# Batch 0 goes from its first to its second stage inside SBUF: twelve small DMAs in place of a round trip through DRAM

## Chip, cores, metric

One core of one Trainium2 chip. The metric is device time in microseconds (us) of one execution. Engines: PE (TensorE, matmuls), DVE (VectorE), ACT (ScalarE), POOL (GpSimd) and SP (SyncE). SP and ACT issue DMAs on their own queues, POOL issues DMAs[...] (the page calls its queue software_dynamic).

## The reference

An FFT over the sequence and over the model dimension, of which the real part is kept, and then a mixture of experts in which each token goes to the one expert with the largest logit.

```python
B, S, D = 8, 2496, 256
x = np.fft.fft(np.fft.fft(x, axis=1), axis=2).real      # per batch
x = x.reshape(B * S, D)                                  # 19968 tokens
logits = x @ w_gate                                      # 8 experts
e = argmax(logits); g = softmax(logits)[e]               # one expert per token
y = g * (relu(x @ w1[e]) @ w2[e])                        # 256 -> 1024 -> 256
```

Tokens are sorted by expert, computed in groups and put back in their places.

## The kernel before

**Stages of a batch.** The length 2496 is split as 104 x 24. The host lays x out so that batch b comes in three loads x(b,q), q = 0 to 2, each 112 rows of 8 KB (896 KB) into a tile `xq`, of which there are three. The *first* stage (`first`) folds mirrored inputs on DVE (an add, L306, and `fold_d`, L295 to L297), and multiplies with the waves `w1` on PE: twelve positions s, four to a load, each an `s` matmul pair of about 104x112 by 104x256 (`half1`; two s share a PSUM tile, ACT copies it into `t1`, L321). The last s needs two tiles, xq and `pm0`. A `t1` of four s is written to DRAM (`Td`, L342, 448 KB), and when all three are there, `regroup` (L354) reads them back in two halves, `t4`, with other rows on the partitions (768 and 640 KB, in rows of 1 KB).

The *second* stage (`second`) starts with `turn_last` (a small matmul `pr` on `t4`, put back into it by ACT, L372), then eleven groups (`p` matmul pairs of `t4` with the constant m2 from `table`, copied to `zz` by ACT, L379) and ten windows of 128 tokens (two `p` matmuls of `zz`, ACT copies `zs` and `lg`, DVE makes `rows`, L410, two of them for each window). After each five windows `route` (L424 to L455) finds the expert and the place of every token (`oh`, the prefix-sum matmuls `rk`, then `pos` and `pi`). The rows then wait in a queue, and `send` writes one set of 128 rows to the sorted array Xs in DRAM by an indirect DMA on POOL (L236, 20 of them for a batch; the short name here is scatter).

**Experts.** `plan` works out on DVE which blocks of a batch are full, SP reads its table and loads weights (`fetch_weights`, 1 MB each for w1 and w2, three buffers each) and rows (`fetch_rows`, `xb` from Xs). `turn` transposes xb (L584, `xT`), then PE runs the `ph` matmuls (xT by w1) and the `py` matmuls (hT by w2). The block list starts with two blocks of 256 rows and four of 128 that need batch 0 alone.

**Order.** The order on each engine is written out by hand: a generator is advanced step by step, and what a step issues stands in each engine's queue at that place. `first(0)` runs alone. Then batch 1's first stage is advanced by `early` (a generator `ahead_of(1)`: twelve steps of `first(1)`, then its regroups): seven steps ahead of `second(0)` and one on every other step of it. Then the experts' generator runs; whenever it yields without work, one step of the side work is issued (planning of batch 0 and what is left of `early`, then batch 2's first and batch 1's second stage). Ahead of the first `turn` it yields nine times, so that nine such steps precede it:

```python
                for _ in range(9):
                    yield 0, False
                for xT in turn(b, size, xbs[0][0]):
                    pass
```

At the head (L949 to L976) ACT loads waves 0 to 3, and SP in this order: x(0,0), x(0,1), the other waves, x(0,2), `table`, `rt`, `wg`, then x(1,0), x(1,1), the regroups of batch 0, x(1,2), `bt` and the padding of Xs. `rt` and `wg` are multiplied (`pg`) into the routing constants.

Of the kernel before, what the change touches and what calls it, by code (L numbers as in the profile page):

```python
# [12 lines left out]
F32 = mybir.dt.float32  # L13
BF16 = mybir.dt.bfloat16
I32 = mybir.dt.int32
ALU = mybir.AluOpType
# [4 lines left out]
B, S, D = 8, 2496, 256  # L21
# [10 lines left out]
HW = NW // 2  # L32
HALF = -(-NG // 2)
LAST = NW * 128 - (NG - 1) * GP
NT = B * S
E, F = 8, 1024
FC = F // 128
# [178 lines left out]
def kernel(ctx: ExitStack, tc, x, w_gate, w1, w2, out):  # L216
# [3 lines left out]
    def mm(o, lhsT, rhs, start=True, stop=True, **kw):  # L220
        nc.tensor.matmul(o, lhsT=lhsT, rhs=rhs, start=start, stop=stop, **kw)  # L221
# [57 lines left out]
    wg = cp.tile([128, 2, E], F32, name="wg")  # L279
    tri = cp.tile([128, 128], BF16, name="tri16")  # L280
    ones = cp.tile([128, 128], BF16, name="ones16")
    waves = const_dram("w1", consts["w1"])

    def load(b, q):

        if b < B:
            xq = xp.tile([NP, 8, D], F32, tag="xq", name="xq", bufs=3)
            row = (b * NQ + q) * NA
            nc.sync.dma_start(out=xq[:].rearrange("p j d -> p (j d)"), in_=x[row:row + NP])
            ahead[b, q] = xq[0:NA]  # L290

    def fold_d(o, a, n):

# [28 lines left out]

    ahead = {}

    def first(b):

        pm0 = xp.tile([NA, D], F32, tag="pm0", name="pm0")
        for q in range(NQ + 1):
            f = iter(())
            if q < NQ:  # L330
                xq = ahead.pop((b, q))
                f = fold(xq, q, pm0[:])
            next(f, None)
            yield
            if q:
                t1 = xp.tile([NP, 4, D], F32, tag="t1", name="t1")
                half1(b, q - 1, 0, pm, pm0, t1)
# [11 lines left out]
    base = con["cap"]  # L349

    def regroup(b, h):
        t4 = sp.tile([128, HALF, D], F32, tag="t4", name="t4")
        n = min(HALF, NG - h * HALF)
        nc.sync.dma_start(  # L354
            out=t4[:, 0:n], in_=bass.AP(Td[b].tensor, Td[b].offset + h * HALF * GP * D,
                                        [[D, 128], [GP * D, n], [1, D]]))
        ahead[b, "t4", h] = t4

    zz = cp.tile([128, 2, NW * 128], F32, name="zz")

    def second(b):
# [368 lines left out]
    def experts(todo):  # L730
# [44 lines left out]
        for k, (b, size, last, at) in enumerate(todo):  # L775
            n, m = size // 128, BIG // size
            if not k:
                while todo[0][:3] not in tabs:
                    yield 0, False
                fetch_some(0, 1)  # L780
                while b not in whole:
                    yield 0, True
                fetch_some(0)
                for _ in range(9):
                    yield 0, False
                for xT in turn(b, size, xbs[0][0]):
                    pass
# [142 lines left out]
    def ahead_of(b):  # L930

        yield from first(b)
        regroup(b, 0)
        regroup(b, 1)

    def mixed(b):

# [9 lines left out]
        yield from through(b)  # L947

    vec.memset(ones[:], 1.0)  # L949
    act.dma_start(out=con["w1"][:, 0:4], in_=waves[:, 0:4])  # L950
    load(0, 0)
    load(0, 1)
    nc.sync.dma_start(out=con["w1"][:, 4:], in_=waves[:, 4:])
    load(0, 2)
    nc.sync.dma_start(out=table[:], in_=const_dram("table", packed))
    nc.sync.dma_start(out=con["rt"][:], in_=const_dram("rt", consts["rt"]))
    nc.sync.dma_start(out=wg[:], in_=w_gate)
    for k in range(WARM):
        pw = pse.tile([128, D], F32, tag="bd"[k % 2], name="py")
        mm(pw[:], ones[:], bc(ones[:], 1, 2))  # L960
# [120 lines left out]
```

## Time and profile before

| | us |
|---|---|
| median of three runs | 1260.61 (1259.76 to 1261.67) |
| the profiled execution | 1258.56 |
| its span, first to last instruction | 1256.8 |
| PE busy in the span | 1208.1 (96%) |
| DVE, ACT, POOL busy | 759.6, 431.3, 447.5 |
| mean granted clock of PE | 0.976 |
| moved by DMA | 249.79 MB, 199 GB/s |

PE is close to full over the span, so the table alone says little of where an edit can act; the page's slices and the windows say in which part of the span PE has room. In the views below, a row of the timeline is start, duration, engine, line, operation, output and input, and in brackets the idle time ahead of it with what ended it; a row of the chain of waits is start, duration and what the time went to; a row of the windows is the stretch, its length, the busy times of PE, PE's weight loads, DVE, ACT and POOL, then the granted clock, the busy share of the DMA engines and GB/s.

### The profile page before, as it was taken

The page shows a single profiled execution, that of the slowest core. Times are in us where ns is not written, and L with a number is a line of the kernel's source. Part 1 is how long each engine was busy: PE and PEld are TensorE (multiplying, and loading weights), DVE is VectorE, ACT ScalarE, POOL GpSimd, SP SyncE. Part 2 cuts the span into 40 slices and gives each one's busy share as a digit, 9 for nine tenths or more (in the row PEclk, how much of TensorE's full clock was granted, in tenths as well). Part 3 has the DMA queues.
Part 4 walks back from the last instruction along what each step waited for, and adds up shares of the span by engine and source line. Part 5 has one row for each costly group of instructions (what it writes and reads, how often), then busy time and mean ns, then how long its engine had stood idle before and what let it go on. Part 6 is the DMA issues. An engine that isn't in the chain of part 4 may idle for free.

```text
span 1256.8 us, 22295 instructions
## 1 busy us (share of the span) xinstructions
PE 1208.1 (96%) x7289; PEld 1076.3 (86%) x7289; DVE 759.6 (60%) x1804; ACT 431.3 (34%) x1167; POOL 447.5 (36%) x527
## 2 busy tenths in 40 slices
PE   5759999999999999999999999999999999999997
PEld 3648998777788899888988899889999999999996
DVE  3455434343456788566866578686888784444653
ACT  1424332333243433434343333442333332222222
POOL 0154527054117522472226603472364241111112
PEclk6869999999999999999999999999999999999998
DMA  8859899873548434673336435453347237878787
GB/s 235 261 174 350 308 317 311 221 237 122 154 153 263 151 110 163 184 234 116 102 124 211 138 96 162 138 180 101 106 139 206 94 105 284 277 285 284 280 292 284
DMA packets 163216, 249.79 MB, mean 199 GB/s; under 512 B 118601, under 2 KB 130227, under 8 KB 143516
## 3 DMA queue, kind: packets, MB, share of 16 engines
q1 hardware_dynamic: 146327, 203.28, 50.7%
q0 software_dynamic: 15888, 42.14, 9.1%
q10 hardware_dynamic: 885, 2.94, 0.7%
q8 instruction: 59, 0.97, 0.3%
q14 instruction: 57, 0.47, 0.1%
HBM read 194.91 MB, written 54.83 MB: 199 GB/s over the span
## 4 chain that ended last, share of the span: by engine, by line
PE 82%; DVE 9%; DMA 4%; ACT 2%; issue 2%; POOL 0%; SPq 0%; POOLq 0%; DVEq 0%; ACTq 0%
PE py L221 25%; PE ph L221 13%; PE a L221 11%; PE c L221 9%; PE p L221 6%; PE b L221 6%; PE d L221 5%; PE e L221 4%; PE s L221 3%; DMA xq<-in_x_dram 1%; DVE xT L584 1%; DMA Td<-t 1%; DVE y L684 1%; DMA Xs<-rows,pi 1%; DVE hT L639 1%
## 5 line engine op out<-in xcount | busy, mean ns | idle before, releaser
L236 POOL DMA_INDIRECT out_dram<-y,ro x163 | 161.4, 990 | 625.3 <-ACT y L680 301.3
L221 PE MATMUL py<-w_sb,hT 128*128 128x256 f32 x1504 | 339.5, 379 | 0.0
L221 PEld LDWEIGHTS py<-w_sb,hT 128*128 128x128 f32 x1504 | 281.4, 190 | 36.9 <-issue 1.0
L236 POOL DMA_INDIRECT Xs<-rows,pi x160 | 162.4, 1015 | 112.0 <-DVE rows L410 56.7
L221 PE MATMUL ph<-xT,w_sb 128*128 128x128 f32 (+2 forms) x992 | 171.1, 328 | 11.2 <-DVE xT L584 11.1
L221 PEld LDWEIGHTS ph<-xT,w_sb 128*128 128x128 f32 x992 | 136.3, 192 | 35.1 <-issue 16.8
L410 DVE SCALAR_TENSOR_TENSOR rows<-p,zs 128x129 f32<-128x129 f32 x160 | 48.9, 348 | 128.8 <-ACT lg L408 124.8
L221 PE MATMUL a<-xT,w_sb 128*128 128x256 f32 (+1 forms) x512 | 117.8, 357 | 0.0
L838 DVE TENSOR_SCALAR hT<-ph 128x512 f32<-128x512 f32 x43 | 29.7, 691 | 123.7 <-PE ph L221 63.7
L587 ACT ACTIVATE xT<-xT 128x256 f32<-128x256 f32 (+1 forms) x94 | 36.5, 388 | 179.2 <-DVE xT L584 140.8
L221 PEld LDWEIGHTS a<-xT,w_sb 128*128 128x128 f32 x512 | 88.6, 190 | 9.7
L892 ACT ACTIVATE y<-py,xb 128x256 f32<-128x256 f32 x94 | 44.6, 475 | 152.2 <-PE py L221 152.2
L636 DVE TENSOR_TENSOR hT<-hT,b 128x512 f32<-128x512 f32 x57 | 39.2, 688 | 75.7 <-PE b L221 50.0
L646 ACT ACTIVATE hT<-a 128x512 f32<-128x512 f32 x57 | 34.0, 597 | 134.1 <-PE a L221 131.1
L221 PE MATMUL s<-xq,w 104*112 104x256 f32 (+2 forms) x208 | 62.8, 425 | 16.3 <-DVE xq L297 12.1
L469 POOL CAST pi<-due 128x1 int32<-128x1 f32 x140 | 45.1, 322 | 65.5 <-ACT due L468 65.5
L221 PE MATMUL a<-w_sb,hT 128*128 128x128 f32 x528 | 66.0, 276 | 0.0
L221 PEld LDWEIGHTS a<-w_sb,hT 128*128 128x128 f32 x528 | 63.1, 192 | 0.7
L221 PEld LDWEIGHTS p<-table,t 120*128 120x128 f32 x352 | 53.6, 202 | 10.6 <-ACT t L372 2.8
L221 PE MATMUL c<-xT,ws 128*128 128x256 f32 (+1 forms) x256 | 60.3, 362 | 1.0 <-DVE hT L642 0.2
L221 PEld LDWEIGHTS s<-xq,w 104*112 104x112 f32 x208 | 38.5, 204 | 26.3 <-DVE xq L297 10.8
L584 DVE STREAM_TRANSPOSE xT<-xb 128x512 f32<-128x512 f32 (+1 forms) x91 | 56.2, 631 | 7.6 <-DMA xb<-Xs 7.6
(149 smaller groups left out, 2072.6 us busy)
## 6 DMA issues: line engine op xcount, KB each, us to landing
w_sb<-in_moe_w_dram SPq DMA_DIRECT2D x132, 1024.0 KB
xq<-in_x_dram SPq DMA_DIRECT2D x24, 896.0 KB
xb<-Xs SPq DMA_DIRECT2D x112, 128.0 KB
Td<-t SPq DMA_DIRECT2D x18, 448.0 KB
t<-Td SPq DMA_DIRECT2D x8, 768.0 KB
t<-Td SPq DMA_DIRECT2D x8, 640.0 KB
xb<-Xs SPq DMA_DIRECT2D x52, 64.0 KB
xb<-Xs SPq DMA_DIRECT2D x88, 32.0 KB
```

The costliest lines, as they stand in the source:

```text
L221: nc.tensor.matmul(o, lhsT=lhsT, rhs=rhs, start=start, stop=stop, **kw)
L236: return unordered(pool.indirect_dma_start(out=dst, out_offset=bass.IndirectOffsetOnAxis(ap=idx, axis=0), in_=rows, in_offset=None, bounds ...
L410: vec.scalar_tensor_tensor(rows[:, k + m, 0:NY], p3[:, 0:NY], zs[:, 0:1], zs[:, 1:], op0=ALU.add, op1=op)
L469: pool.tensor_copy(idx, due[:])
L584: vec.transpose(free(xT[:], 256 * h, [32, n // 32], [BIG, 2], [1, 32]), free(xb, 512 * h, [64, n // 32], [1, 2], [2, 32]))
L587: act.activation(odd, odd, ACTF.Copy, scale=-1.0)
L636: vec.tensor_tensor(h12, h11, b[:], op=add)
L639: vec.tensor_tensor(h21, h12, d[:], op=add)
L646: act.activation(h11, a[:], ACTF.Relu)
L684: vec.tensor_tensor(o, o, p[:], op=add)
L838: vec.tensor_scalar(o, ph[:], 0.0, None, op0=ALU.max)
L892: act.activation(y[:, i % 2], py[:], ACTF.Copy, scale=meta[:, i, 1:2])
```

## The change

1. Batch 0 has its own first stage, `first_whole`, in half loads (two s at a time: half the add, half the fold, two s). Its waves come in another column order (`wp`, 110 columns, in a buffer of the second weights), so that row r of the result belongs to group r % 11. For each s one DMA on ACT's queue (the last on SP's) then takes `t1` straight to its place in `t4s`: ten partitions, s, s + 12, ..., each with eleven rows of 1 KB. `Td` and the regroups of batch 0 are gone.
2. `t4s`, one tile with both halves, takes the place of the two `t4` buffers for all batches.
3. The waves in their old order, which batches 1 to 7 use, are made from `wp` by three copies on POOL (`natural`), and the two unused columns are set to zero by DVE.
4. The waves come in three parts and x(0,2) in two, in turn on SP. `table`, `rt` and `wg` move to POOL's queue, behind a copy (`came`) that waits for the last waves. x(1,0), x(1,1), `bt` and the padding also move to POOL's queue; x(1,2) stays on SP.
5. `early` gives three steps ahead of `second(0)`, not seven, and inside it none until its fifth step (k = 4). x(2,2) is loaded after the regroups of batch 1, not in `first(1)`.
6. Twelve steps, not nine, precede the first `turn`.

```diff
+NR = 2 * NU * NG
...
-    waves = const_dram("w1", consts["w1"])
+    wp = bp.tile([128, NS + 3, NR], F32, tag="w2", name="wp", bufs=3)[0:NA]
+    order = consts["w1"][:, :, 0:NR].reshape(NA, NS + 3, NG, 2 * NU).swapaxes(2, 3)
+    waves = const_dram("w1", order.reshape(NA, NS + 3, NR))
...
+    def first_whole():
+        pm0 = xp.tile([NA, D], F32, tag="pm0", name="pm0")
+        for q in range(NQ):
+            xq = ahead.pop((0, q))
+            t1 = xp.tile([NP, 4, D], F32, tag="t1", name="t1")
+            for lo in (0, 2):
+                end = q == NQ - 1 and lo
+                a, m = xq[:, lo:lo + 2], xq[:, 4 + lo:6 + lo]
+                n = 2
+                if end:
+                    n = 1
+                    fold_d(pm0[:], m[:, 1], 1)
+                vec.tensor_tensor(a[:, 0:n], a[:, 0:n], m[:, 0:n], op=ALU.add)
+                fold_d(m, a, 2)
+                ps = pm_.tile([NP, 2, D], F32, tag="m", name="s1")
+                for i in range(2):
+                    s = 4 * q + lo + i
+                    o = ps[0:NR, i]
+                    if s < NS - 1:
+                        mm(o, columns(s), m[:, i])
+                        continue
...
+                if end:
+                    for i in range(2):
+                        act.copy(t1[0:NR, lo + i], ps[0:NR, i])
+                else:
+                    act.copy(t1[0:NR, lo:lo + 2], ps[0:NR])
+                for i in range(2):
+                    s = 4 * q + lo + i
+                    (nc.sync if s == NS - 1 else act).dma_start(out=t4s[s:GP:NS, 0:NG], in_=t1[0:NR, lo + i])
+            load(1, q, queue=nc.sync if q == NQ - 1 else pool)
+        for h in range(2):
+            ahead[0, "t4", h] = t4s[:, h * HALF:(h + 1) * HALF]
...
+    def natural(lo, hi):
+        n = hi - lo
+        pool.tensor_copy(free(con["w1"][:, lo:hi], 0, [NP, n], [2 * NU, NG], [1, 2 * NU]),
+                 free(wp[:, lo:hi], 0, [NR, n], [1, NG], [NG, 2 * NU]))
...
-                if b:
+                if b > 1 or b and q < NQ:
                     load(b + 1, q - 1)
...
-        t4 = sp.tile([128, HALF, D], F32, tag="t4", name="t4")
+        t4 = t4s[:, h * HALF:(h + 1) * HALF]
...
-                for _ in range(9):
+                for _ in range(12):
                     yield 0, False
...
         regroup(b, 1)
+        if b == 1:
+            load(b + 1, NQ - 1)
...
-    act.dma_start(out=con["w1"][:, 0:4], in_=waves[:, 0:4])
+    vec.memset(con["w1"][:, :, NR:], 0.0)
+    act.dma_start(out=wp[:, 0:4], in_=waves[:, 0:4])
     load(0, 0)
     load(0, 1)
-    nc.sync.dma_start(out=con["w1"][:, 4:], in_=waves[:, 4:])
-    load(0, 2)
-    nc.sync.dma_start(out=table[:], in_=const_dram("table", packed))
-    nc.sync.dma_start(out=con["rt"][:], in_=const_dram("rt", consts["rt"]))
-    nc.sync.dma_start(out=wg[:], in_=w_gate)
+    nc.sync.dma_start(out=wp[:, 4:8], in_=waves[:, 4:8])
+    rest = load(0, 2, 2)
+    next(rest)
+    nc.sync.dma_start(out=wp[:, 8:], in_=waves[:, 8:])
+    next(rest)
+    came = cp.tile([1, 1], F32, name="came")
+    pool.tensor_copy(came[:], wp[0:1, NS + 2, 0:1])
+    pool.dma_start(out=table[:], in_=const_dram("table", packed))
+    pool.dma_start(out=con["rt"][:], in_=const_dram("rt", consts["rt"]))
+    pool.dma_start(out=wg[:], in_=w_gate)
...
-    for _ in first(0):
-        pass
-    load(1, 0)
-    load(1, 1)
-    regroup(0, 0)
-    regroup(0, 1)
-    load(1, 2)
-    nc.sync.dma_start(out=bt[:], in_=const_dram("blocks", cv))
-    sent(unordered(nc.sync.dma_start(
+    first_whole()
+    pool.dma_start(out=bt[:], in_=const_dram("blocks", cv))
+    sent(unordered(pool.dma_start(
...
+    for lo in range(0, NS + 3, 5):
+        natural(lo, lo + 5)
...
-    for _ in range(7):
+    for _ in range(3):
         next(early)
     for k, _ in enumerate(second(0)):
-        if k % 2 == 0:
+        if k > 3 and k % 2 == 0:
             next(early, None)
```

More of the change, by code (lines that the diff above doesn't have):

```diff
@@ L281, with load @@
     ones = cp.tile([128, 128], BF16, name="ones16")
-    waves = const_dram("w1", consts["w1"])
-    def load(b, q):
+    wp = bp.tile([128, NS + 3, NR], F32, tag="w2", name="wp", bufs=3)[0:NA]
+    order = consts["w1"][:, :, 0:NR].reshape(NA, NS + 3, NG, 2 * NU).swapaxes(2, 3)
+    waves = const_dram("w1", order.reshape(NA, NS + 3, NR))
+    def load(b, q, parts=1, queue=nc.sync):
         if b < B:
@@ L288, in load, with pieces @@
             row = (b * NQ + q) * NA
-            nc.sync.dma_start(out=xq[:].rearrange("p j d -> p (j d)"), in_=x[row:row + NP])
             ahead[b, q] = xq[0:NA]
+            if parts == 1:
+                queue.dma_start(out=xq[:].rearrange("p j d -> p (j d)"), in_=x[row:row + NP])
+                return iter(())
+            return pieces(xq, row)
+    def pieces(xq, row):
+            for k in range(2):
+                nc.sync.dma_start(
+                    out=xq[:].rearrange("p (c j) d -> p c j d", c=2)[:, :, 2 * k:2 * k + 2],
+                    in_=x[row:row + NP].rearrange("p (c j d) -> p c j d", c=2, d=D)[:, :, 2 * k:2 * k + 2])
+                yield
     def fold_d(o, a, n):
@@ L323, with columns @@
     ahead = {}
+    def first_whole():
[19 more added lines that the diff above has]
+                        continue
+                    for k, l, r in ((NS - 1, 0, H + 1), (NS + 1, H + 1, D)):
+                        mm(o[:, l:r], columns(k), pm0[:, l:r], True, False)
+                        mm(o[:, l:r], columns(k + 1), m[:, 1, l:r], False, True)
+                if end:
[9 more added lines that the diff above has]
+            ahead[0, "t4", h] = t4s[:, h * HALF:(h + 1) * HALF]
+    def columns(s):
+        return wp[:, s]
+    def natural(lo, hi):
+        n = hi - lo
+        pool.tensor_copy(free(con["w1"][:, lo:hi], 0, [NP, n], [2 * NU, NG], [1, 2 * NU]),
+                 free(wp[:, lo:hi], 0, [NR, n], [1, NG], [NG, 2 * NU]))
     def first(b):
@@ L357, in regroup @@
         ahead[b, "t4", h] = t4
+    t4s = cp.tile([128, 2 * HALF, D], F32, name="t4s")
     zz = cp.tile([128, 2, NW * 128], F32, name="zz")
```

## Prediction

> **What bounds the kernel now.** First the page's 40 slices, for where TensorE is not full, then the windows for its head and its rest.
>
> ```profile
> PE   5759999999999999999999999999999999999997
> PEclk6869999999999999999999999999999999999998
> ...
> 0.00:89.50 89.50, 52.34 (x246) 40.69 (x246) 43.57 (x155) 25.00 (x80) 22.56 (x24) 0.71 0.76 230
> ...
> 89.50:1256.80 1167.30, 1155.78 (x7043) 1035.64 (x7043) 716.08 (x1650) 406.26 (x1087) 424.92 (x503) 1.00 0.60 196
> ```
>
> After 89.5 us TensorE is busy for 1155.8 of 1167.3 us at full clock: from there the time is its work. Only the head has room: 37 us idle, and a mean granted clock of 0.71. So the change is worth what it takes from the start of the first expert block, plus what PE work it brings ahead of that start. Next, the chain of waits through the head:
>
> ```profile
> 0.75 7.64 DMA xq<-in_x_dram
> ...
> 15.51 10.59 DMA Td<-t
> ...
> 27.27 3.61 DMA Td<-t
> ...
> 32.05 8.97 DMA xq<-in_x_dram
> ...
> 57.11 5.44 DMA t<-Td
> ...
> 82.36 2.48 DMA Xs<-rows,pi
> ...
> 88.79 0.72 DVE xT L584
> ...
> 89.55 3.66 PE ph L221 x8
> ```
>
> and four rows of the timeline that mark the stages, with PE's waits in the head:
>
> ```profile
> 35.83 0.57 PE L221 MATMUL pr<-t,table 120*120 120x6 f32 x2 [1.24 <-DMA t<-Td]
> 54.08 0.17 DVE L453 TENSOR_TENSOR pi<-pf,table 128x10 int32<-128x10 f32 x1
> 55.19 1.11 POOL L236 DMA_INDIRECT Xs<-rows,pi  x1 [54.73 <-DVE rows L410]
> 62.68 0.54 PE L221 MATMUL pr<-t,table 120*120 120x6 f32 x2 [0.20 <-DMA t<-Td]
> ...
> PE ph L221 <- DVE xT L584: 11.1, 1, 11.1
> ```
>
> The reader is to see: batch 0's first stage is through the matmuls at 26, but the last Td write lands at 30.88 and its second stage starts (pr) at 35.83. Its route gives the first indices at 54.25; 20 scatters on POOL run from 55.19 to 83.3; the last lands at 84.84, xb at 88.67, and `ph` starts at 89.55, after 11.1 us without PE work. The scatters set the pace: 55.19 to 89.55 is 34.4 us, 20 x 1.27 us being 25.4 of it.
>
> [...] the first Td write, 448 KB on ACT's queue, took 10.59 us, while 283 GB/s x 10.6 us = 3.0 MB were moved, which is about all that SP had issued before it (rest of x(0,2), tables, x(1,0)). I take the measurement: a transfer waits for the backlog ahead of it. [...] a scatter takes 0.97 us, but 2.03 when it starts at 65.53 beside the add of a fold (65.51). [...]
>
> **The change part by part.**
>
> *Batch 0's fold in halves.* x(0,0) lands at 8.4 as before. Half an add and half a fold_d are 0.6 + 0.35 + 0.35 + 0.1 = 1.4 us (half of 1.23, 0.69, 0.68, 0.17), against 2.7 before the first matmul at 11.10: first matmul 9.9, first copy (four matmuls, 1.9, and 0.6) ends at 12.4. x(0,2) comes in two pieces with no table in front: 182 KB (1.76 KB rows) + 448 after 11.7, at 250 GB/s 14.3, the rest 17. pm0 (0.75), add, fold: 19.2; last matmuls 22.5 (before 26), last copy 23.2.
>
> *Twelve DMAs for three Td writes and two regroups.* 3 x 448 KB written and 1408 KB read go; 12 x 110 KB come. Each costs ACT about 0.31 us of issue (as the Td rows), 11 x 0.31 = 3.4 us between copies that wait for PE anyway. When the last lands is what counts. With everything issued ahead of it (w 0.69 MB, five x loads 4.59, tables 0.71, t4s 1.35) 7.3 MB must pass; before, 6.4 MB had passed at 26.1 (211 GB/s to 10, 231 to 15.5, then 3.0 MB), so at 283 GB/s 7.3 MB is reached at 29.5. Bounds: 25.5 if the small DMAs overtake x(1,1) (issue 23.3 and 2.2 us), 38 or later if they go one by one (rival D). I take **29.5**: second(0) starts 6.3 us earlier.
>
> *POOL's queue.* `came` waits for the last waves (about 16), then come table, rt, wg, x(1,0), x(1,1), bt, pad: seven DMAs at about 1 us (nearest row: 0.97), done near 23 to 26. Behind them three copies `natural` of 550 elements[...]. First user: the s matmuls of batch 1, about 37. First scatter behind them: 47. Cover 10 us; without it each us is one. Table and rt are needed at 26 to 29, and land by about 21. x(1,0) must be folded before the first `rows` (29.5 + 5.3); landing by 28 to 30 + 2.75 it is just in time.
>
> *Fewer steps of batch 1 ahead (3 for 7, and none until its fifth step (k = 4)).* Before, `rows` waited for x(1,2) until 41.05. In the changed order only x(1,0)'s fold lies ahead of the first `rows`; x(1,1)'s fold (2.7) lies between them and x(1,2)'s add (0.75 + 0.95) between the reciprocal and `pos`. pr to first rows 5.3 (4.2 of matmuls and copies as at 35.83 to 43.8 without the s matmuls, 1.1 p3 and copy), five windows 6.7 with the folds, route 3.4 + 1.7: 17.1 for the 18.4 of before. First indices **46.6**, before 54.25. Scatters then 47.6, and with the same 34.4 us `ph` by this chain at **82.0**.
>
> *What is late next: batch 1.* Its last s matmuls now stand behind batch 0's second rk. 46.6 + 7.8 (54.25 to 62.02) + 1.5 (fold_d) = 55.9; matmuls and copies 3.3; Td write 5.4 (51.73 to 57.11); regroup 5.4: pr(1) at **70.0**, before 62.68. In the PE order, ahead of the first `ph`, stand pr, two p pairs (2.4), three s pairs and five windows: 2.4 + 2.2 + 5 x 1.65 (71.1 to 77.7 held four) = 13: `ph` at **83**. SP has the regroups, x(2,2) and both weights in that order: from 64.6, 2.36 + 2.1 MB at 283 to 350 GB/s, w1 at 74 to 77, w2 at 77 to 80; xb, issued near 77, waits behind it. I take `ph` at **84**.
>
> *Twelve steps for nine.* Three more steps, less two that early still owes: one s pair (0.9 at full clock) and one group with its window (0.95) are ahead of the first `ph`; they stood behind it. From the first 128-row `ph` on both orders are the same. Gain **1.85**.
>
> *Edits at nothing.* The memset of two columns of the waves lies in DVE's idle time up to 8.41. wp takes one of three w2 buffers; it is free once `natural` has run (under 40), the third weights were fetched at 100. The third t1 must wait for the first four t4s DMAs: issued by 14.5, they need the backlog of then (about 17 to 19) and are wanted at 18.9; before, the same wait was 6.6 us, and 2 us of it would be inside the bound of 25.5 to 29.5. t4s holds two halves as the two t4 buffers did: batch 1's regroup waits for batch 0's last read near 54, and is issued at 64.6.
>
> *Sum.* 89.55 - 84 = 5.55, + 1.85 = 7.4. The first eight `ph` ran at half clock (3.66 for 1.8): if PE arrives warm, up to 1.8 more; I count nothing. The profiled execution, 1258.56 (span 1256.8), becomes 1251.2; the median is 2.05 above it: **1253.2**.
>
> **Rivals.**
> A (forecast): both chains end at 82 to 84; 0.48.
> B: batch 1 is not late (the t4s land at 25.5 to 28), the scatters alone decide and PE arrives warm: 89.55 - 81 + 1.85 + 1.8 = 12.2, 1248.4. For it: small DMAs; against: 10.59 for the first Td write. 0.22.
> C: the DMA engines take it back. From 105 to 135 their share is 1.02 at 360 GB/s; an earlier start meets the same weights, and PE has never waited for weights there, so the slack is unknown. `ph` at 88 or waits of 3 to 4 us: gain 3, 1257.6; 0.16.
> D (slower): the DMAs on ACT's queue come one after the other. At 2.48 us each (a scatter's landing) 12.6 + 12 x 2.48 = 42.4; batch 1's chain makes `ph` = t4s + 54.5 = 97. It decides from `ph` = 91.4, that is t4s at 36.9. 1260.6 + 5.5 = 1266; 0.09. Against: four xb DMAs issued at 85.08 to 87 landed within 3.6 us together.
> E: the DMAs only replace the round trip's time: 1260; 0.05.
>
> **How the numbers follow.** Likeliest 1253.2. 0.2% is 2.5 us, about what a measurement can tell. Faster: 0.47 of A, B, 0.10 of C = 0.79; same 0.12; slower 0.09 (D). The range takes B with a little more at one end and E at the other: 1247.5 to 1260.
>
> **What would show it.** pr of batch 0 at 29.5 (25.5 to 32), first scatter 47.6, pr of batch 1 at 70, first `ph` at 84, PE's wait for xT from 11.1 to under 4 us, span less by as much plus 1.85. Wrong if pr comes after 36, if `ph` waits for something other than these two chains, or if PE shows new waits for weights from 95 to 160.

## The result and the profile after

The changed kernel takes 1267.36 us (median of 6 runs, 1266.19 to 1269.25), the kernel before 1260.20 beside it (6 runs, 1255.78 to 1261.67): ratio 1.0065, 95% interval 1.0053 to 1.0077. A second measurement of the same two kernels (f0 below) gave 1.0077 (1.0060 to 1.0094). The change makes the kernel 0.65% slower, where the forecast was 7 us faster (1253.2, range 1247.5 to 1260.0).

The profiled execution took 1269.2 us with a span of 1267.2 (before 1258.56 and 1256.8). The slices of the page, and then the windows, cut at the first `ph` (same columns as before):

```profile
PE   4658999999999999999999999999999999999997
PEclk7778999999999999999999999999999999999999
```

```profile
0.00:98.40 98.40, 52.65 (x258) 42.56 (x258) 52.13 (x181) 27.28 (x88) 30.49 (x35) 0.75 0.68 194
98.40:1267.20 1168.80, 1156.30 (x7031) 1034.51 (x7031) 713.15 (x1638) 404.21 (x1081) 425.67 (x503) 1.00 0.60 196
```

The span grew by 10.4 us. Of these 8.9 lie ahead of the first `ph` (89.55 before, 98.41 now) and 1.55 behind it (1167.25 before, 1168.80 now). So the place is the one that the prediction named, the head, with the other sign. The chain of waits through it (start, duration, what):

```profile
9.72 2.06 PE s L222 x4
...
23.01 2.88 PE s L222 x10
...
26.32 12.90 DMA t4s<-t
...
70.85 3.11 DMA Td<-t
...
74.02 6.13 DMA t4s<-Td
...
84.96 8.90 DMA Xs<-rows,pi
...
95.65 1.92 DMA xb<-Xs
...
98.42 6.49 PE ph L222 x16
```

and PE's waits in the head (us in total, times, longest):

```profile
PE pr L222 <- DMA t4s<-t: 11.6, 1, 11.6
PE pr L222 <- DMA t4s<-Td: 10.1, 1, 10.1
PE s L222 <- DMA t4s<-t: 5.7, 1, 5.7
...
PE ph L222 <- DVE ro L853: 4.5, 1, 4.5
```

Three things are to be seen. The last but one `t4s` DMA of batch 0 is issued at 26.32 and not at 23.3, and it lands 12.90 us later: `pr` starts at 39.52, before the change at 35.83. The first scatter starts at 58.10 (before 55.19). And the last scatter takes 8.90 us to land where it took 2.48. Before, `ph` waited 11.1 us for its transposed input; now the wait there is 4.5 us, but `pr` of batch 0 and of batch 1 wait 11.6 and 10.1 us.

**Where the 12.90 us went.** Three stretches of 2 us of this execution, by queue (packets, MB, share of the 16 engines; q0 is POOL's queue, q10 ACT's, q1 SP's). From 24 to 26:

```profile
q0 software_dynamic: 63, 0.42, 93.5%
q10 hardware_dynamic: 36, 0.04, 10.0%
```

From 30 to 32:

```profile
q10 hardware_dynamic: 256, 0.24, 55.9%
q1 hardware_dynamic: 42, 0.20, 51.4%
q0 software_dynamic: 30, 0.07, 10.2%
```

From 34 to 36:

```profile
q1 hardware_dynamic: 52, 0.36, 62.2%
q10 hardware_dynamic: 46, 0.04, 9.2%
```

From 22 to 28 ACT's queue moves 34, 36 and 41 packets per 2 us, rows of 1 KB, while POOL's moves 63, 63 and 71, 176 of these 197 being 8 KB rows of x(1,0) and x(1,1): 0.11 MB of `t4s` in 6 us beside 1.45 MB of x. Counted in packets, ACT's queue has 0.54, 0.57 and 0.58 for one of POOL's. ACT's eleven `t4s` DMAs are 1320 packets in all (12 to 40): 1210 rows and ten short ones for each DMA.

The last row of x(1,1) moves at 29.7. So all x that had been issued ahead is through when the prediction's sum said (29.5), but at 30 us 450 of the 1210 small rows are not. From 30 to 32 they go fast (256 packets). Then x(1,2) stands in their way, though SP issued it at 27.71, behind the last `t4s` (26.32 on ACT, 26.59 on SP): 46 packets beside 52 from 34 to 36, and the last small row moves at 38.7. The `t4s` DMAs did not wait for the backlog ahead of them to pass, nor did they overtake it: for one packet of another queue they moved 0.54 to 0.58 beside POOL's and 0.88 beside SP's (46/52), which was issued later, and most of those packets were eight times as large.

### The profile page after: what moved, and what is told of

The parts are those of the page before. It is cut to its first block, busy times and chain, and to the rows that moved or that the text cites. A ratio compares the mean times of both kernels' runs of the same rounds, so it can differ in the third digit from the quotient of the medians.

```text
span 1267.2 us, 22328 instructions
## 1 busy us (share of the span) xinstructions
PE 1208.9 (95%) x7289; PEld 1077.1 (85%) x7289; DVE 765.3 (60%) x1817; ACT 431.5 (34%) x1168; POOL 456.2 (36%) x538
## 3 DMA queue, kind: packets, MB, share of 16 engines
q0 software_dynamic: 16448, 44.95, 10.1%
## 4 chain that ended last, share of the span: by engine, by line
PE 80%; DVE 8%; DMA 5%; ACT 2%; issue 2%; SPq 1%; ACTq 1%; POOL 0%; POOLq 0%; DVEq 0%
PE py L222 23%; PE ph L222 12%; PE a L222 11%; PE c L222 9%; PE p L222 6%; PE b L222 6%; PE d L222 5%; PE e L222 4%; PE s L222 3%; DVE xT L644 1%; DMA t4s<-t 1%; DMA xb<-Xs 1%; DVE y L744 1%; DMA w_sb<-in_moe_w_dram 1%; DMA Xs<-rows,pi 1%
## 5 line engine op out<-in xcount | busy, mean ns | idle before, releaser
L222 PEld LDWEIGHTS py<-w_sb,hT 128*128 128x128 f32 x1504 | 281.4, 190 | 36.9 <-issue 1.0
L898 DVE TENSOR_SCALAR hT<-ph 128x512 f32<-128x512 f32 x43 | 29.7, 691 | 131.5 <-PE ph L222 71.6
L696 DVE TENSOR_TENSOR hT<-hT,b 128x512 f32<-128x512 f32 x57 | 39.2, 687 | 75.3 <-PE b L222 49.6
L222 PEld LDWEIGHTS p<-table,t4s 120*128 120x128 f32 x352 | 54.7, 205 | 8.8 <-issue 2.6
L222 PE MATMUL p<-table,t4s 120*128 120x120 f32 (+1 forms) x352 | 57.6, 290 | 1.9 <-ACT t4s L432 1.9
L222 PE MATMUL p<-table,zz 128*128 128x145 f32 (+1 forms) x320 | 56.7, 301 | 2.4 <-ACT zz L439 1.3
L222 PE MATMUL c<-xs,ws 128*128 128x256 f32 (+1 forms) x256 | 58.8, 357 | 0.0
```

What stands on the lines that cost most here:

```text
L696: vec.tensor_tensor(h12, h11, b[:], op=add)
L898: vec.tensor_scalar(o, ph[:], 0.0, None, op0=ALU.max)
```

## The experiments

Kernels with the same number under "before beside it" ran on one chip together with that kernel. Its median differs from chip to chip, so ratios are compared, and in the profiles only the heads. One caution: the stretch from the first `ph` to the end took 1167 to 1173 us in the profiles of the chips where the kernel before has 1259 to 1260, but 1176 to 1192 on the other three (e1 to e4, the i and the j runs), where no profile of the kernel before was taken. A ratio there can't be traced to the head alone. `pr`, `pr(1)` and `ph` are the first `pr` of batch 0, that of batch 1 and the first `ph`.

| run | pr | first scatter | pr(1) | ph | median, us | before beside it | ratio and interval |
|---|---|---|---|---|---|---|---|
| before | 35.83 | 55.19 | 62.68 | 89.55 | | | |
| after | 39.52 | 58.10 | 80.29 | 98.41 | 1267.36 | 1260.20 | 1.0065 (1.0053 to 1.0077) |
| e1_small_rows | 35.44 | 53.35 | 77.86 | 95.98 | 1282.38 | 1273.20 | 1.0068 (1.0047 to 1.0089) |
| e2_loads_last | 29.80 | 48.65 | 73.54 | 90.61 | 1277.34 | 1273.20 | 1.0023 (0.9999 to 1.0046) |
| e3_two_queues | 37.02 | 55.44 | 82.98 | 100.12 | 1277.74 | 1273.20 | 1.0022 (1.0006 to 1.0038) |
| e4_nine | 37.70 | 55.81 | 84.01 | 98.43 | 1284.31 | 1273.20 | 1.0073 (1.0056 to 1.0089) |
| f0_changed_again | 38.46 | 56.16 | 80.17 | 98.41 | 1268.37 | 1258.81 | 1.0077 (1.0060 to 1.0094) |
| f2_weights_cut | 30.33 | 52.88 | 76.08 | 94.14 | 1262.64 | 1258.81 | 1.0023 (1.0011 to 1.0035) |
| e6_both | 29.86 | 49.59 | 72.07 | 88.97 | 1260.32 | 1258.81 | 1.0013 (1.0001 to 1.0024) |
| e5_before_twelve | 34.02 | 53.24 | 62.91 | 87.77 | 1258.42 | 1258.81 | 0.9999 (0.9990 to 1.0008) |
| h1_early_again | 38.58 | 57.93 | 79.22 | 102.39 | 1277.36 | 1259.08 | 1.0146 (1.0129 to 1.0162) |
| h2_no_pause | 29.78 | 55.66 | 73.32 | 91.81 | 1261.97 | 1259.08 | 1.0022 (1.0011 to 1.0033) |
| h3_no_pause_nine | 29.82 | 55.87 | 73.68 | 91.58 | 1263.04 | 1259.08 | 1.0028 (1.0016 to 1.0040) |
| f3_early_two | 40.00 | 58.98 | 79.82 | 102.97 | 1277.70 | 1259.08 | 1.0147 (1.0132 to 1.0163) |
| i1_gate | 37.96 | 55.40 | 81.20 | 98.44 | 1292.02 | 1287.85 | 1.0040 (1.0017 to 1.0062) |
| i2_both_gate | 26.66 | 45.04 | 77.17 | 95.26 | 1280.18 | 1287.85 | 0.9947 (0.9930 to 0.9965) |
| i3_tables_sp | 28.36 | 50.38 | 74.99 | 91.69 | 1280.50 | 1287.85 | 0.9937 (0.9917 to 0.9957) |
| i4_gate_nine | 26.59 | 45.24 | 70.15 | 86.48 | 1283.21 | 1287.85 | 0.9973 (0.9953 to 0.9993) |
| j1_both_gate_again | 27.47 | 46.00 | 76.50 | 94.47 | 1269.32 | 1273.56 | 0.9964 (0.9944 to 0.9984) |
| j2_tables_sp_again | 27.53 | 46.72 | 71.03 | 88.24 | 1272.57 | 1273.56 | 0.9998 (0.9979 to 1.0016) |

### Which of them holds the small DMAs back

Theory T: what a queue gets beside another goes by packets and not by bytes ("turns" for short), so that rows of 8 KB hold back rows of 1 KB. Rivals: B, the bytes ahead must pass; S, the small copies are slow in themselves. That rows of x(1,2), issued behind, went in between (46 packets beside 52) speaks against B already.

**e1_small_rows**: the three loads of batch 1, each in four DMAs of 1 KB runs.

```diff
+    def small(b, q, queue):
...
+        for k in range(4):
+            queue.dma_start(
+                out=xq[:].rearrange("p (c j) d -> p c j d", c=2)[:, :, k:k + 1],
+                in_=x[row:row + NP].rearrange("p (c j d) -> p c j d", c=2, d=D)[:, :, k:k + 1])
...
-            load(1, q, queue=nc.sync if q == NQ - 1 else pool)
+            small(1, q, nc.sync if q == NQ - 1 else pool)
```

> Edit on the changed kernel: the three loads of batch 1's x are each cut into four DMAs with runs of 1 KB instead of 8 KB; same queues, same place, same bytes. Theory T ([...] a 1 KB row of t4s gives way to an 8 KB row of x): the last t4s lands near 31 to 33, not 39.2, batch 0's pr starts there, first ph near 90 to 92 (98.4), time near 1260. Theory S (the twelve small DMAs are slow by themselves[...]): pr stays near 39, time 1267. Theory B (what counts is the bytes ahead in the backlog): same bytes, pr stays near 39, time 1267.

From 24 to 26, the stretch shown above for the changed kernel, the two queues of this run stood so:

```profile
q0 software_dynamic: 157, 0.45, 86.8%
q10 hardware_dynamic: 95, 0.09, 20.2%
```

With the same bytes in front, ACT's queue got 2.6 times as many packets (95 for 36). For one packet of POOL's it had 0.61 (95/157), in the changed kernel 0.57 (36/63): much the same ratio, with smaller packets. That speaks for T and against B and S. But `pr` at 35.44 missed the expected 31 to 33. The runs of 1 KB did not become packets of 1 KB on POOL's queue: 157 packets carry 0.45 MB, some 3 KB each (on SP's queue, where x(1,2) goes, 195 carry 0.18 MB from 30 to 32, about 1 KB each). So these packets came down from 8 KB to some 3 on average and not to 1; what joins the runs isn't shown. And part of what `pr` gained is not the turns: the last ACT issue came at 23.59 instead of 26.32. (Why, i1 shows.) The time didn't move.

**e2_loads_last**: all loads of batch 1 on SP, behind the last `t4s`.

```diff
-            load(1, q, queue=nc.sync if q == NQ - 1 else pool)
+        for q in range(NQ):
+            load(1, q)
```

> Edit on the changed kernel: all three loads of batch 1's x go on SP's queue behind the last t4s, none on POOL's. T: with nothing but the end of x(0,2) and the tables beside them the t4s land as they are issued, pr of batch 0 at 29 to 31, first ph near 90, time 1258 to 1260. S: pr at 36 or later, time 1264 or more. B: pr near 29, as T.

`pr` comes at 29.80, with the last issues at 26.28 and 26.55 as before: the last DMAs land within 3.5 us of their issue, with no x ahead of them in the queues. In the same 24 to 26 ACT's queue alone carries

```profile
q10 hardware_dynamic: 92, 0.08, 14.1%
```

all that had been issued. S falls here. The ratio is 1.0023, against 1.0065 and 1.0077 for the changed kernel, so the x rows in the way are the larger part of the slowdown; f2 below, which holds this edit, has 1.0023 beside 1.0077 on one chip. B expects the same of e2: that it is the turns and not the bytes rests on e1 and on the counts of packets.

**e3_two_queues**: every second `t4s` on SP's queue, with the loads on POOL's.

```diff
-                    (nc.sync if s == NS - 1 else act).dma_start(out=t4s[s:GP:NS, 0:NG], in_=t1[0:NR, lo + i])
+                    (nc.sync if s % 2 else act).dma_start(out=t4s[s:GP:NS, 0:NG], in_=t1[0:NR, lo + i])
```

> Edit on the changed kernel: every second t4s goes on SP's queue, so that ACT issues six and not eleven. The issue of one takes ACT 0.79 us, and the last goes out at 26.3. T: SP's queue is one more with turns, so the small rows get about twice the share beside x, and the last is issued 2 to 3 us earlier: pr near 34, time near 1262. S (engine time of the small rows): 2 to 3 us at most, pr near 37, time 1264 to 1265.

A miss: 37.02 where 34 was expected. The two small queues got 30 and 25 packets from 24 to 26, 38 and 38 from 26 to 28, so together 1.5 and 1.9 times those of ACT's in the changed kernel (POOL's moved 55 from 24 to 26: each small queue has 0.55 and 0.45 packets for one of POOL's), and yet `pr` was only 2.5 us earlier than in the changed kernel. The ratio of 1.0022 is better than a `ph` at 100.12 explains; one profile and 12 executions, on a chip with a longer rest, do not settle that.

### Which of them holds ph

**f0_changed_again**: the changed kernel, as a control.

> The changed kernel itself, unaltered, beside the kernel before and the three others of this set, so that their differences can be read on one chip. Every theory: 1.0065 of before, first ph about 9 us later than before.

It repeats: 1.0077, `ph` at 98.41. The chain of waits goes through batch 1's `Td` write and regroup (71.00 and 74.14) instead of the scatter's landing, so the two chains end together.

**e4_nine**: the changed kernel with nine steps ahead of the first `turn`.

```diff
-                for _ in range(12):
+                for _ in range(9):
```

> Edit on the changed kernel: nine steps ahead of the first turn, as before, not twelve. If the prediction's step holds (the three steps bring 1.85 us of PE work into idle time ahead of ph): first ph stays near 98.4 and the time grows by 1.5 to 2 us, to 1269. Rival: the steps themselves hold ph up (they stand ahead of it in PE's and DVE's order): ph earlier by 1 us or more, time the same or less than 1267.

**e5_before_twelve**: the kernel before with twelve.

```diff
-                for _ in range(9):
+                for _ in range(12):
```

> Edit on the kernel before: twelve steps ahead of the first turn instead of nine, nothing else. If steps there bring PE work into the 11 us without PE ahead of the first ph: three steps more of about 0.9 us each at full clock, ph at 89.5 to 90.5, time 1.5 to 2.5 us less than before. Rival: x(2,2) and batch 1's chain stand ahead of the transposition then, ph comes later by as much, time the same or more.

Neither moves the time: 1.0073 against 1.0068 and 1.0077 of the twelve, and 0.9999 (0.9990 to 1.0008) for the kernel before. In e5 `ph` is 1.8 us earlier (87.77) although more stands ahead of it, since `pr` was 1.8 us earlier too (34.02): in that execution the DMAs ahead of it came sooner. In e4 the distance from `pr(1)` to `ph` is 14.4 us instead of 18.1, but the rows from Xs aren't there (PE waits 4.7 us for xT), and `ph` starts at the same 98.4. Both chains hold `ph`, and taking away the three steps alone brings nothing.

What the twelve steps put ahead of the transposition in DVE's order, in the changed kernel (start, duration, engine, line, operation):

```profile
93.08 0.28 DVE L309 TENSOR_TENSOR pm<-xq 104x127 f32<-104x127 f32 x1
...
93.55 0.95 DVE L320 TENSOR_TENSOR xq<-xq 104x768 f32<-104x768 f32 x1
94.42 0.61 DVE L470 SCALAR_TENSOR_TENSOR rows<-p,zs 128x129 f32<-128x129 f32 x2
94.94 0.23 DVE L484 TENSOR_REDUCE mx<-lg 128x10 f32<-128x80 f32 x1
...
96.39 0.68 DVE L309 TENSOR_TENSOR xq<-xq 104x508 f32<-104x508 f32 x1
96.98 0.68 DVE L310 TENSOR_TENSOR xq<-xq 104x508 f32<-104x508 f32 x1
97.58 0.17 DVE L311 COPY xq<-xq 104x8 f32<-104x8 f32 x1
97.66 0.70 DVE L644 STREAM_TRANSPOSE xT<-xb 128x512 f32<-128x512 f32 x1
```

The fold of batch 2's x(2,2), the rows of the fifth window and the start of batch 1's route take 93.08 to 97.66; PE ran out of work at 93.95. PE's wait there is 4.5 us, and it is 4.5 in e2, e6, i1, i2, i3, j1 and j2 as well. In this execution `xb` lands at 97.57, just as DVE is through, so either of the two would have held `ph` here. In i2 and j1 SP issues `xb` at 80.2 and 80.5, over 13 us ahead of the transposition (94.50 and 93.71), and the wait is the same: there DVE's order alone holds it.

**f2_weights_cut**: e2, and the first block's weights in 1 KB runs, so that the last scatter's rows shouldn't wait for 8 KB rows of weights.

```diff
+        cut = 4 if first_block else 1
+        for k in range(cut):
+            f = slice(k * F // cut, (k + 1) * F // cut)
+            nc.sync.dma_start(out=w1_sb[:, :, f], in_=w1[ds(ev, 1)].rearrange("o p c f -> p (o c) f")[:, :, f])
```

> Edit on the kernel with the loads of batch 1's x behind the last t4s (all on SP): the two weight loads of the first block, 1 MB each, are cut into four DMAs with runs of 1 KB instead of 8; same place and bytes. It asks where the second delay comes from: there the last scatter of batch 0 took 7.2 us to land and xb 5.9 (before: 2.48 and 3.7). T (packet turns): rows of Xs and xb get a fair turn beside the weights, the last scatter lands within 4 us, first ph 3 to 4 us earlier than the 90.6 of that kernel, time 3 us less. Rival (the bytes of weights, x(2,2) and regroups queued ahead): landing stays 6 us or more, ph at 90, time unchanged.

A miss: the 20th scatter was issued at 79.36 and `xb` at 85.53, so its landing still took about 6 us (7.2 in e2). Turns by the size of rows do not explain this landing. SP also spent 6.74 us on issuing the four pieces of w2 here, which spreads the weights over the same stretch, so the run does not separate turns from bytes. What lengthens the landing in the changed kernel, the regroups, x(2,2) or both weights in flight together from 74 to 92, stays open.

**e6_both**: e2 and e3 together.

```diff
-                    (nc.sync if s == NS - 1 else act).dma_start(out=t4s[s:GP:NS, 0:NG], in_=t1[0:NR, lo + i])
-            load(1, q, queue=nc.sync if q == NQ - 1 else pool)
+                    (nc.sync if s % 2 else act).dma_start(out=t4s[s:GP:NS, 0:NG], in_=t1[0:NR, lo + i])
+        for q in range(NQ):
+            load(1, q)
```

> Edit on the changed kernel: loads of batch 1's x behind the last t4s on SP, and every second t4s issued by SP, so that ACT's share of the issue time falls from 8.7 to 4.7 us. With no x beside the small rows, the issue is what is left: last t4s issued near 23.5 and not 26.3, pr of batch 0 at 27 (29.8 with the loads moved alone), first scatter near 46, ph near 88, time 2 to 3 us below the kernel with the loads moved alone. Rival: SP's queue holds the small rows back as ACT's did, and pr stays near 29.5.

A miss at `pr` (29.86, expected 27): the last ACT issue stays at 26.39 though ACT issues half as many. The ratio is 1.0013 (1.0001 to 1.0024). This run is the forecast's own case: `pr` near the predicted 29.5, and yet `ph` at 88.97, not 84, and no gain.

**h2_no_pause** (e6, and a step of batch 1 on every even k) and **h3_no_pause_nine** (h2 with nine steps):

```diff
-        if k > 3 and k % 2 == 0:
+        if k % 2 == 0:
```

> Edit on the kernel with batch 1's loads last and the small DMAs on two queues (1.0013 of before): early gives a step on every even k of second(0), not from k = 4 on. C1: batch 1's last s matmuls stand ahead of the second rk and its regroups go out 3 to 5 us earlier; pr of batch 1 near 68 (72.1), first ph near 86 (89.0), where the scatters hold it; 0.998 to 0.9995 of before. C2: ph stays at 89, or later by the folds that now stand ahead of rows; 1.0013 or more.

> Edit on the kernel with a step on every even k: nine steps ahead of the first turn, not twelve. The three steps stand ahead of the transposition on DVE (a window's rows, the start of a route, a fold), so ph comes 1 to 3 us earlier; the 1.85 us of PE work that they bring ahead of ph goes behind it. Expected: first ph near 84, time the same as with twelve steps within 1.5 us. Rival (the steps are worth their PE work in full): ph not earlier, time 1.5 to 2 us more.

Both miss. The first `rows` of batch 0 now stand on DVE behind the folds of x(1,0) and of x(1,1), whose x has not come: in h2 these start at 34.45 and 37.76, and the first `rows` at 41.43 instead of 36.86 (e6). The first scatter slips to 55.66 and 55.87, and `ph` to 91.81 and 91.58. With x loaded this late the pause of part 5 is needed.

**h1_early_again** (the changed kernel with part 5 undone) and **f3_early_two** (e6 with part 5 undone). In both, batch 1's regroup is written into `t4s` ahead of batch 0's last groups, so these read rows of batch 1 and the routing of batch 0 is another; their total times can't be compared with the rest.

```diff
-                if b > 1 or b and q < NQ:
+                if b:
...
-        if b == 1:
-            load(b + 1, NQ - 1)
...
-    for _ in range(3):
+    for _ in range(7):
...
-        if k > 3 and k % 2 == 0:
+        if k % 2 == 0:
```

> Edit on the changed kernel: part 5 of the change undone (seven steps of batch 1 ahead of second(0), one on every even k, x(2,2) inside first(1)); everything else as changed, x(1,0) and x(1,1) on POOL's queue as there. It asks which chain holds the first ph. Theory C1 (batch 1's chain: its Td write and regroups, then 17 to 18 us from pr of batch 1 to ph): pr of batch 0 stays near 38 to 39, but pr of batch 1 falls from 80 to 66 or less and first ph from 98.4 to 92 to 94, where the scatters then hold it; time 1261 to 1263 on a chip where the changed kernel has 1268. Theory C2 (the scatters hold it, batch 1's chain is only beside): ph stays at 97 or more, time as the changed kernel.

> Edit on the kernel with batch 1's loads last and the small DMAs on two queues: part 5 of the change undone (seven steps ahead, all even k, x(2,2) inside first(1)). Batch 1's folds then stand ahead of batch 0's second stage, and its x lands at 31 to 38: pr of batch 0 at 36, first rows near 42 (before 43.8), first scatter near 52.5 (55.2), batch 1's chain as early as before. C1 and C2 alike: first ph near 87, 0.998 of before. If the t4s and not the waits for x had been the gain, it is gone: 1.000 or more.

PE waits 13.0 and 12.4 us for the regroup inside batch 0's groups. They show what the pause protects: with one tile for all batches (part 2), batch 1 can't run further ahead. Part 5 undone beside separate tiles was not tried.

### Why the last DMA is issued late

In the changed kernel, and in most of those with its order, the last fold of x(0,2) looked odd. DVE and POOL in the changed kernel:

```profile
17.97 1.37 DVE L352 TENSOR_TENSOR xq<-xq 104x256 f32<-104x256 f32 x1
19.38 1.24 DVE L309 TENSOR_TENSOR xq<-xq 104x254 f32<-104x254 f32 x1
20.54 1.35 DVE L310 TENSOR_TENSOR xq<-xq 104x254 f32<-104x254 f32 x1
21.81 1.10 DVE L311 COPY xq<-xq 104x4 f32<-104x4 f32 x1
```

```profile
19.46 0.83 POOL L1037 DMA_DIRECT2D Xs<-pad  x1
20.27 3.75 POOL L381 COPY w<-wp 104x550 f32<-104x550 f32 x3
```

The same four instructions (L352 to L311) take 0.42, 0.42, 0.42 and 0.16 us in i1 below. They end 3.6 us late, about what the three `natural` copies take, though by the records the stretching begins some 2 us ahead of these (spans on POOL are rough). Theory G: POOL's work holds DVE up.

**i1_gate**: the changed kernel with a small copy on POOL that waits for this fold, ahead of bt, the padding and `natural`.

```diff
                 fold_d(m, a, 2)
+                if end:
+                    late = cp.tile([1, 1], F32, name="late")
+                    pool.tensor_copy(late[:], m[0:1, 1, 0:1])
```

> The changed kernel, with one small POOL copy of a number of the last folded x(0,2) put ahead of bt, the padding and the three natural copies, so that POOL does these after DVE's last fold and not beside it. Theory G (POOL's copies and DMA issues stretch DVE's last fold: subtractions of 254 took 0.42 us before 18 us and 1.24 to 1.36 beside POOL): the last fold ends at 19.5 to 21 instead of 22.9, the last t4s DMA of ACT is issued at 23 to 24.5 instead of 26.3. With theory T (turns with the 8 KB rows of x) on top, pr hardly moves: 37 to 38.5. Rival N (PE's or ACT's own pace sets the last issue): last fold or last issue unchanged. Time: ratio to the kernel before 1.005 to 1.008 by T, 1.003 if pr follows the issue.

The same rows of DVE, in i1:

```profile
17.90 0.42 DVE L352 TENSOR_TENSOR xq<-xq 104x256 f32<-104x256 f32 x1
18.35 0.42 DVE L309 TENSOR_TENSOR xq<-xq 104x254 f32<-104x254 f32 x1
18.69 0.42 DVE L310 TENSOR_TENSOR xq<-xq 104x254 f32<-104x254 f32 x1
19.02 0.16 DVE L311 COPY xq<-xq 104x4 f32<-104x4 f32 x1
```

This shows that POOL's work held DVE: the four rows took 5.06 us beside it, 1.42 with it behind them. Of that work bt, the padding and the copies were moved, so which of them did it is not told apart; the issues of x(1,0) and x(1,1) stayed (18.00 to 19.13) beside rows of usual length, so it is not these. The fold ends at 19.18 instead of 22.91 and ACT's last `t4s` goes out at 23.68 instead of 26.32, as G has it. But `pr` comes at 37.96: with the x rows in the way, the DMA that is issued 2.6 us earlier waits 1.1 us longer.

```profile
23.68 13.97 DMA t4s<-t
```

Beside e1, with the same issue (23.59) and `pr` at 35.44, this also sizes what the cut rows did there by themselves: 2.5 us (two executions of one kernel, the changed one and f0, differ by 1.1 at `pr`).

**i2_both_gate**: e6 with the same copy, that is, without the x rows and without the held DVE.

> e6_both with the same small copy. Here no 8 KB rows are in the way of the t4s DMAs, so G expects the whole gain at pr: last issue 23.3 to 24 instead of 26.4, pr 26.5 to 27.5 instead of 29.9, first scatter 46 to 47, first ph 85.5 to 87 instead of 89.0, time 0.9980 to 0.9995 of the kernel before. Rival N: pr stays at 29.5 to 30, time 1.001.

```profile
26.66 0.54 PE L222 MATMUL pr<-t4s,table 120*120 120x6 f32 x2 [2.25 <-issue]
```

`pr` 26.66 and the first scatter at 45.04, where G expected 26.5 to 27.5 and 46 to 47: 12.9 us ahead of the changed kernel's `pr`, 3.2 ahead of e6. The ratio is 0.9947 (0.9930 to 0.9965): faster than the kernel before. `ph` missed (95.26 for 85.5 to 87): ACT stood idle for 8.36 and 5.16 us before copying batch 1's last `t`, and so the `Td` write, the regroup and `pr(1)` came late.

**i3_tables_sp**: i2 with `table`, `rt` and `wg` back on SP. **i4_gate_nine**: i3 with nine steps.

```diff
-    came = cp.tile([1, 1], F32, name="came")
-    pool.tensor_copy(came[:], wp[0:1, NS + 2, 0:1])
-    pool.dma_start(out=table[:], in_=const_dram("table", packed))
-    pool.dma_start(out=con["rt"][:], in_=const_dram("rt", consts["rt"]))
-    pool.dma_start(out=wg[:], in_=w_gate)
+    nc.sync.dma_start(out=table[:], in_=const_dram("table", packed))
+    nc.sync.dma_start(out=con["rt"][:], in_=const_dram("rt", consts["rt"]))
+    nc.sync.dma_start(out=wg[:], in_=w_gate)
```

> i2_both_gate with table, rt and wg back on SP, behind the last piece of x(0,2), and without the copy came: POOL has nothing to do until the last fold. G: no fold of batch 0 is stretched, last fold ends near 19.4, last issue near 23; the 0.69 MB of tables now share the DMA engines with the t4s DMAs, so pr 26 to 28; time within 0.1% of i2_both_gate. Rival: table rows of some KB hold the t4s as the rows of x did: pr 29 or later.

> i3_tables_sp with nine steps ahead of the first turn, as before the change. The last fold of x(2,2), a route start and one window leave DVE's order ahead of the transposition: from pr of batch 1 to ph 14 to 15 us instead of 17, ph near 84 unless the last scatter's landing and xb hold it (then 86). Time equal to i3_tables_sp within 0.1%, since work that goes ahead of ph is missing behind it; if an earlier ph counts by itself, 2 us less.

i3 gives 0.9937 (0.9917 to 0.9957), i4 0.9973 (0.9953 to 0.9993). In i4 `ph` is at 86.48, held by xb (PE waits 7.9 us for xT), in i3 at 91.69. Nine for twelve was expected to change nothing; here the intervals only just overlap, and the runs of i4 spread from 1276.64 to 1292.94.

**j1_both_gate_again**, **j2_tables_sp_again**: i2 and i3 once more.

> The kernel of i2_both_gate once more. Its profile showed pr at 26.7 and the first scatter at 45.0 as theory G has it, but then ACT without work for 8.4 and 5.0 us (53 to 67) for a cause that the profile does not name, so ph came at 95.3 only. If that was an accident of the one execution: no such gap, pr of batch 1 near 68 to 70, ph 85 to 87. Ratio to the kernel before 0.9945 if the first measurement holds, 0.9975 to 0.9990 by the head alone (2.5 to 4.5 us of 89.6, less 1 us of half clock after it).

> The kernel of i3_tables_sp once more. pr 26.5 to 28.5, ph 86 to 91 (rows of batch 0 wait for x(1,0), which stands behind the tables). Ratio to the kernel before 0.9937 if the first measurement holds, 0.9980 to 1.0010 by the head alone.

i2's kernel is faster again, 0.9964 (0.9944 to 0.9984); i3's is not, 0.9998 (0.9979 to 1.0016). The gap on ACT was no accident of one execution:

```profile
66.76 0.59 ACT L335 COPY t<-s 112x512 f32<-112x512 f32 x1 [5.85 <-remote]
```

comes again in j1 ("remote" is a releaser that the profile can't name), and `ph` at 94.47. So two profiles of this kernel show a late `ph`, while its medians are 4 to 8 us under the kernel before. The medians are measured and the version is faster; how it gains what it gains isn't shown. No profile of a typical execution of it was had (the profiled ones took 1288.92 and 1276.86, medians 1280.18 and 1269.32), and both have 1191.7 and 1180.5 us behind `ph`, where e6 has 1167.0: on these chips the gain need not lie in the head. What stops ACT stays open too. Of the versions tried, i2 is the only one that was under the kernel before in two measurements.

## Why the prediction was wrong, step by step

**The landing of the t4s: the step that failed.** The prediction read "a transfer waits for the backlog ahead of it" from one 448 KB write of 10.59 us. That reading was not forced. The write was issued at 15.51, and its first packet moves at 20.1. All that the queues moved from 16 to 20 in the kernel before is SP's:

```profile
q1 hardware_dynamic: 399, 0.92, 102.7%
```

From 20 to 24 the write moved 99 rows of 4 KB beside 104 of 8 KB, 0.95 for one:

```profile
q1 hardware_dynamic: 147, 0.87, 67.1%
q10 hardware_dynamic: 102, 0.41, 32.0%
```

So the 10.59 us are a wait of 4.6 (the first `t4s` has one too: issued at 12.42, its first row moves at 15.86) and then a share by packets; what the wait is for stays open. Of the 3.0 MB of that stretch 0.66 were ACT's own. The write thus allowed a share by packets from 20 on, and the reading that was chosen gave 29.5 for small rows where 39.2 was measured. It left out the size of the rows and x(1,2), which is issued later. The 2.2 us of its lower bound (25.5) were the author's estimate; in the kernel before, the last scatter landed in 2.48 us and an `xb` in 1.98. "Wrong if pr comes after 36" was the right alarm. Rival D had the side and the break-even right (`pr` behind 36.9 makes it slower) with another mechanism (one DMA after the other), and was given 0.09.

**The issues.** 11 x 0.31 us were counted, from Td's 4 KB rows. Measured is 0.79 to 0.91 us for each on ACT:

```profile
12.42 1.74 ACTq L371 DMA_DIRECT2D t4s<-t  x2
...
26.32 0.79 ACTq L371 DMA_DIRECT2D t4s<-t  x1
```

8.8 us instead of 3.4 in ACT's order. The last issue was late by 3 us through POOL's work beside the last fold, though, not through this: i1 has the same eleven issues and the last at 23.68.

**POOL's queue, "edits at nothing".** As a matter of due dates `natural` was hidden: POOL was through at 24.0, and the first user (s of batch 1) came at 48.5. The step missed that POOL's work can hold DVE up: beside it the four instructions of the last fold took 5.06 us, in i1, with bt, the padding and the copies behind it, 1.42. The three copies took 1.25 us each and the delay was 3.6 us, so the sizes agree. By what means POOL's work held DVE, and whether the copies did it or bt or the padding, was not shown.

**pr to the first indices:** predicted 17.1, measured 17.7 (39.52 to 57.2). **t4s to pr(1):** predicted 40.5, measured 40.8. Both right for the changed kernel; the second is the cost of part 5, since before it was 26.85. (With `pr` at 29.8 it was 43.7 in e2 and 42.2 in e6.)

**pr(1) to ph:** predicted 13, measured 18.1, and 16.7 to 18.5 in all other runs with twelve steps that kept parts 2 and 5 as they are or undid only the pause (e1 to e3, e6, f0, f2, h2, i1 to i3, j1, j2). The sum counted PE's instructions of the three added steps and not DVE's: the fold of x(2,2) and the route's start, ahead of the transposition, where PE waits 4.5 us (with `xb` as late in the changed kernel, by DVE alone in i2 and j1). This term alone takes the forecast away: with 17.5, the middle of these, 29.5 + 40.8 + 17.5 = 87.8 against 89.55 leaves 1.8 us, and e2 and e6, with `pr` at 29.8, measured `ph` at 90.61 and 88.97 and no gain.

**First scatter to ph:** "the same 34.4", measured 40.3. Issuing took as long (26.9 us against 27.2); the last landing went from 2.48 to 8.90, while SP's regroups, x(2,2) and weights are in flight; f2 did not show which of them does it, or how. The prediction had seen that xb would wait for the weights, but had not put it on the scatters.

**Twelve steps, 1.85 us:** not there. In e5 the kernel before with twelve measured 0.9999 (0.9990 to 1.0008). That what goes ahead of `ph` also delays it, through DVE or PE, fits this, but e5's one profile, with `pr` 1.8 us earlier, does not show it.

**Behind ph:** the prediction counted nothing, with up to 1.8 us of gain if PE ran at full clock there. It ran at half: a granted clock of 0.50 for 5.6 us from the first `ph`, against 3.4 before. Eight `ph` took 3.66 us at that clock in the kernel before and 1.74 after it, so by an estimate from these (half of 5.6 less 3.4) the longer stretch is some 1.1 of the 1.55 us that the rest is longer.

## What to carry to other kernels

Ahead of a small DMA that something waits for, count the packets of the other queues and not only the bytes, those issued behind it too (36 small ones went beside 63, and 46 beside 52 of a load issued later); hold the large load until the small ones are out (e2, `pr` at 29.80 for 39.52), or cut it and look in the trace at what size its packets have (e1, some 3 KB for runs of 1). A copy moved to an engine "with room" is free only if it doesn't hold up the engine on the path; look beside it for instructions whose duration trebles (0.42 us to 1.24 and more here). And where two chains end together, cost the order on every engine that the last step passes, DVE here, since a step moved ahead on PE brings its DVE work along.

## What the runs showed of the hardware

- Rows of 1 KB on ACT's queue beside rows of 8 KB on POOL's got 34 to 41 packets in 2 us (0.54 to 0.58 for one of POOL's) and 7.6 to 10% of the engines' time, and 46 beside 52 of SP's queue with x(1,2), which had been issued later. Beside POOL's packets of some 3 KB they got 95 (e1, 24 to 26, 0.61 for one), and with no x in the queues 627 in 4 us beside 120 of POOL's (e2, 20 to 24).
- A load with runs of 1 KB went in packets of some 3 KB on POOL's queue (157 for 0.45 MB, 24 to 26) and of about 1 KB on SP's (195 for 0.18 MB, 30 to 32), both in e1.
- The issue of a DMA from SBUF to SBUF of 110 rows of 1 KB held ACT for 0.79 to 0.91 us and SP for 0.92, one from SBUF to DRAM of 112 rows of 4 KB held ACT for 0.31 or 0.32.
- Beside POOL's copies of 550 elements and the DMA issues ahead of them, four DVE instructions took 5.06 us together; with that work moved behind them (i1), 1.42.
